# The first hundred microseconds of a spectral-filter and SiLU kernel: other transfers, another order of loads, products of zeros

## The chip, the cores and the metric

The kernel runs on one core of a Trainium2 chip. The metric is the device time of one execution in microseconds; five executions of the kernel before give a median of 2637.14 us (2634.81 to 2638.34). The profile shows one execution. Its engines are TensorE (PE, with its weight loads PEld), VectorE (DVE), ScalarE (ACT), GpSimd (POOL) and SyncE (SP), which here only issues transfers.

## The reference

`x` has 8 batches of 3008 positions and 256 channels. Each batch is filtered in the frequency domain along the positions, and the result goes through a two-layer network:

```python
X = np.fft.rfft(x, axis=1)
Y = X * (filt_r + 1j * filt_i)[None]          # 1505 frequencies x 256 channels
y = np.fft.irfft(Y, n=3008, axis=1).astype(np.float32)
h = y.reshape(24064, 256) @ w_in              # w_in 256 x 2048
out = (h / (1 + np.exp(-h)) @ w_out).astype(np.float32)   # w_out 2048 x 256
```

`x` and the filters are float32. The weights arrive as 64-bit floats (their scale is a float64), and the kernel rounds them itself.

## The kernel before

**The spectral part.** The transform of length 3008 = 47 x 64 is done in stages, each a set of small matrix products with tables (`wf_t`, `d_t`, `e_t`, `wi_t`). For batch 0, and in the same way for batch 1, with other timing:

- `load_x(u)` (L255), for 8 blocks u. A block holds on partitions 0 to 46 and on 64 to 110 the rows 32 apart of both halves of the positions. Each half of a block (`h`) comes in two transfers, of 32 and of 15 rows, all on the Sync queue. Rows 32 to 63 of the tile are filled with zeros first, since `sums` reads rows 0 to 110.
- `sums(u)` (L280): sum and difference of the two halves, two VectorE instructions.
- `stage1(u)` (L294): eight TensorE passes with `wf_t`, two evictions to `t1`, and two writes on GpSimd's queue to the DRAM scratch `d1`. `evac` (L226) gives evictions to ScalarE in batch 0 (`early[0]` is set), and to VectorE and ScalarE in turn after that.
- `load_t2(g)` (L377), for 6 groups g: two transfers on the Sync queue read `d1` back, transposed. All of `d1` has to be written before the first. `forward(g)` (L383) multiplies with `d_t`, and at its end issues the load of group g + 2, as there are two `t2` tiles.
- `multiply(g, k)` (L399) by the filters on VectorE, `add(g, k)` (L408) on GpSimd in batch 0 but for one half of the last group, `inverse(g)` (L414) with `e_t` on TensorE, and then `even` (a ScalarE copy) and `rows` (two VectorE instructions), which writes to the DRAM scratch `d2`, in batch 0 nearly always by ScalarE's queue.
- `load_t4(g)` (L450) reads `d2` back once all of it is written; `stage3(g)` (L456) multiplies with `wi_t`, issues the load of group g + 2 and evicts to `y`.

From batch 2 on the first stage is folded for six of the eight blocks (`load_fold`, `fold`, `stage1_fold`), and only blocks 6 and 7 come by `load_x`.

**The weights.** `load_weights(jp)` (L700) loads two of the 16 columns of 128 hidden units as raw 64-bit words, four transfers of 256 KB. `round_weights(j)` (L714) turns one column into float32: five VectorE and two ScalarE instructions and two GpSimd products, and after every second column four GpSimd combinations.

**The main loop.** 384 steps: 8 batches, two halves each, three runs of tokens each, 8 pairs of hidden columns each. Both layers are multiplied as 2 x 2 blocks with seven products instead of eight. `hidden(step)` (L566) issues the first layer's seven products and the SiLU of one pair, in 8 rounds; `project` (L625) the second layer's products of the step before. The pieces of the next batch's spectral part are placed between them by step and round (`plan`, L487): batch 1's `sums(u)` at step u, round 5, and its `stage1(u)` at step u + 1, round 3. The roundings of columns 9 to 15 lie in steps 0 to 5.

**The order around the change.** The schedule is written by hand: each engine's instructions, and each queue's transfers, stand in the order in which the program calls them (L774 to L861). Transfers of the Sync and ScalarE queues share eight completion counters, and a transfer waits until the previous one on its counter has landed, so at most eight are under way. The start-up of batch 0 (L774 to L819) is: all of x; d_t; raw weights of jp 0; the first third of the filters (Sync queue); the first stage; the rest of the filters (GpSimd's queue); t2 of groups 0 and 1; e_t; two roundings; the six groups; t4; the roundings of columns 4 to 8; four groups of stage 3. Then the main loop's first product is issued (`px`, L579 and L586).

Of the kernel before, what the change touches and what calls it, by code (L numbers as in the profile page):

```python
# [155 lines left out]
def kernel(  # L156
# [47 lines left out]
    f_t = [cpool.tile([128, NG, 2, C], FP32, name=f"filt{i}") for i in range(2)]  # L204

    w_t = cpool.tile([128, 7, 2, NJP, 128], FP32)
    warm = cpool.tile([128, 1], FP32)
    bias_t = cpool.tile([128, 1], FP32)
    x_all = xpool.tile([128, 2, 2, 2 * C], FP32)
# [39 lines left out]
    def spectral(b):  # L249
# [5 lines left out]
        def load_x(u):  # L255


            if b == 0:
                if u == 0:
                    us["t1"] = gpool.tile([128, 2, 2, 2, C], FP32, name="t1_g", tag="g")  # L260
                if u in (0, 2):
                    xs["y"] = ypool.tile([128, 2, HALF], FP32, name=f"x_{b}_{u}", tag="y")
                if u < 4:
                    xs[u] = xs["y"][:, u % 2, 0:1024].rearrange("p (a n) -> p a n", a=2)
                elif u < 6:
                    xs[u] = t4pool.tile([128, 2, 2 * C], FP32, name=f"x_{b}_{u}", tag="t4")
                else:
                    xs[u] = x_t[u % 2]
                (nc.vector, nc.gpsimd)[u % 2].memset(xs[u][32:64], 0.0)
            else:  # L270
                xs[u] = x_t[u % 2]
            for h in range(2):
                for r0, nr in ((0, 32), (32, N1 - 32)):
                    nc.sync.dma_start(
                        out=xs[u][64 * h + r0:64 * h + r0 + nr],
                        in_=bass.AP(tensor=x.tensor,
                                    offset=x.offset + (b * S + 32 * r0 + 4 * u + 2 * h) * C,
                                    ap=[[32 * C, nr], [32 * N1 * C, 2], [1, 2 * C]]))
# [15 lines left out]
        def stage1(u):  # L294
            ut = us.pop(u)
            if b > 0 or u < 2 or u > 5:
                t1 = tpool.tile([128, 2, 2, C], FP32, name=f"t1_{b}_{u}", tag="t")
            elif u < 4:
                t1 = typool.tile([128, 2, 2, C], FP32, name=f"t1_{b}_{u}", tag="ty")
            else:  # L300
                t1 = us["t1"][:, u - 4]
            ps = [bank(b, f"pa_{b}_{u}_{h}") for h in range(2)]
            for par in range(2):
                for h in range(2):
                    rows = slice(64 * h, 64 * h + N1)
                    nc.tensor.matmul(out=ps[h][64 * par:64 * par + 64], lhsT=wf_t[rows, par],  # L306
                                     rhs=ut[rows, par], start=True, stop=True)
            for h in range(2):
                evac(t1[:, h], ps[h])
            for par in range(2):  # L310
                nc.gpsimd.dma_start(
                    out=d1[par].rearrange("s p n c -> (s p) n c")[:, 4 * u:4 * u + 4, :],
                    in_=t1[64 * par:64 * par + 2 * NS].rearrange("p h n c -> p (h n) c"))
# [61 lines left out]
                        in_=us["tf"][32 * k:32 * k + NS].rearrange("p q n c -> p (q n) c"))  # L375

        def load_t2(g):  # L377
            t2s[g] = tpool.tile([128, 4, C], FP32, name=f"t2_{b}_{g}", tag="t")
            for par in range(2):
                nc.sync.dma_start(out=t2s[g][64 * par:64 * par + 64],  # L380
                                  in_=d1[par, 4 * g:4 * g + 4].rearrange("s p n c -> (p n) s c"))

        def forward(g):  # L383
            t2 = t2s.pop(g)
            ps = [bank(b, f"pb_{b}_{g}_{k}") for k in range(2)]
            for ri in range(2):
                for j in range(4):
                    for k in range(2):
                        par, at = slot_source(k, j)
                        rows = slice(64 * par, 64 * par + 64)  # L390
                        nc.tensor.matmul(out=ps[k][32 * j:32 * j + 32, ri, :],  # L391
                                         lhsT=d_t[rows, 4 * g + at, ri, :], rhs=t2[rows, at, :],
                                         start=True, stop=True)
            if g + 2 < NG:
                load_t2(g + 2)
            banks[g] = ps
            prods[g] = []
# [50 lines left out]
                queue.dma_start(out=d2[a0:a0 + 4].rearrange("a n h c -> (a n) h c"), in_=qt[:, a])  # L448

        def load_t4(g):  # L450
            t4s[g] = t4pool.tile([128, 4, C], FP32, name=f"t4_{b}_{g}", tag="t4")
            for h in range(2):
                nc.sync.dma_start(out=t4s[g][64 * h:64 * h + 2 * NS],
                                  in_=d2[:, 4 * g:4 * g + 4, h, :])

        def stage3(g):  # L456
            half, n0 = divmod(4 * g, 16)
            ps = [bank(b, f"pd_{b}_{g}_{h}").rearrange("p a c -> p (a c)")[:, 0:8 * N1]
                  .rearrange("p (a i n) -> p a i n", a=2, i=4) for h in range(2)]
            for cb in range(2):  # L460
                for i in range(4):
                    for c0 in (0, 64):
                        for h in range(2):
                            rows = slice(64 * h, 64 * h + 2 * NS)
                            nc.tensor.matmul(  # L465
                                out=ps[h][c0:c0 + 64, cb, i, :],
                                lhsT=t4s[g][rows, i, 128 * cb + c0:128 * cb + c0 + 64],
                                rhs=wi_t[rows, :], start=True, stop=True)
            if g < 6:
                load_t4(g + 2)  # L470
            if n0 == 0:
                y[b, half] = ypool.tile([128, 2, HALF], FP32, name=f"y_{b}_{half}", tag="y")
            dst = y[b, half].rearrange("p a (r h n) -> p a h n r", h=2, n=16)
            for h in range(2):
                evac(dst[:, :, h, n0:n0 + 4], ps[h])
# [204 lines left out]

    wide = moe_w_in.dtype != FP32
    nc.vector.memset(warm, 0.0)
    nc.scalar.activation(out=warm, in_=warm, func=AFT.Silu)

# [74 lines left out]
    def rounded(j):  # L761
        if wide:
            round_weights(j)
        else:
            load_exact(j)

    def inverse_rows(part, g):
        part["inverse"](g)
        for i in range(2):
# [2 lines left out]


    nc.sync.dma_start(out=wf_t, in_=wf_dram.ap())  # L774
    nc.gpsimd.memset(bias_t, -896.0)
    nc.gpsimd.memset(x_all[96:128], 0.0)
    part = spectral(0)
    for u in range(8):
        part["load_x"](u)
    nc.sync.dma_start(out=d_t, in_=d_dram.ap())  # L780
    weights(0)
    load_filters(nc.sync, 0, 4)
    for u in range(3):
# [1 line left out]
    for u in range(8):  # L785
        part["stage1"](u)
        if u + 3 < 8:
            part["sums"](u + 3)
    load_filters(nc.gpsimd, 4, 2 * NG)
    part["load_t2"](0)  # L790
    part["load_t2"](1)
    nc.sync.dma_start(out=e_t, in_=e_dram.ap())
    rounded(0)
    rounded(1)
    for g in range(NG):
        part["forward"](g)
        if g == 0:
# [7 lines left out]
            part["add"](g, k)  # L805
        if g > 0:
            inverse_rows(part, g - 1)
        if g in (1, 3):
            rounded(2 + g // 2)
    inverse_rows(part, NG - 1)  # L810
    weights(4)
    part["load_t4"](0)
    part["load_t4"](1)
    for j in range(4, 9):
        rounded(j)
        if j == 5:
# [74 lines left out]
```

## Time and profile before

| What | Value |
|---|---|
| Median of five executions | 2637.14 us |
| The profiled execution | 2637.78 us, span 2635.6 us |
| TensorE busy | 2561.2 us, 97% of the span |
| VectorE, ScalarE, GpSimd busy | 1717.0, 1101.1, 491.9 us |
| TensorE busy in the first 120 us | 63.9 us |
| First product of the main loop | at 114.22 us |
| Bytes moved in the first 130 us | 27.35 MB, 210 GB/s on average |
| Mean granted clock of TensorE | 0.987 |

Part 1 of the page gives busy time, share and number of instructions of each engine. Part 2 cuts the span into 40 slices; a digit is the busy share in tenths. A line of the chain of waits has a start, a length and the work or wait that the end was traced back to. A line of the timeline has a start, the length of the whole group, engine, line, operation, tile written and tile read, the count, and in square brackets the idle time before the group with what ended it; `SPq` and `ACTq` are queues issuing transfers. A line of the windows has a stretch, its length, busy time and number of instructions of PE, PEld, DVE, ACT and POOL, the granted clock, the busy share of the 16 DMA engines, and GB/s. Tiles are called by the kernel's names without numbers: `t` is any of `t1`, `t2`, `t4`; `d` is `d1` or `d2`.

The granted clock reads 1.00 from the start, although the eight passes of a first-stage block take 2.48 us at 14.41 us and 1.09 at 134.56; so the column is no measure in the first 60 us.

### The profile page before, as it was taken

The numbers are of one execution on the slowest core, as the hardware profiler recorded it, in microseconds if no ns is written. First come the engines' busy times: TensorE is split into PE (matmuls) and PEld (weight loads), VectorE is DVE, ScalarE is ACT, GpSimd is POOL, SyncE is SP. The second block draws the span as 40 slices with busy tenths as digits, with TensorE's granted clock in tenths as the row PEclk, the third lists the DMA queues.
The fourth block names the chain that finished last, engine by engine and source line by source line (L and its number), as shares of the span: only waits on it lengthen the run. The fifth ranks groups of instructions, "written<-read, shape, count | busy, mean of one in ns | idle before, by whom it ended". The sixth has DMA issues, their size and how long they took to land.

```text
span 2635.6 us, 48160 instructions
## 1 busy us (share of the span) xinstructions
PE 2561.2 (97%) x18720; PEld 2164.0 (82%) x18720; DVE 1717.0 (65%) x3578; ACT 1101.1 (42%) x3012; POOL 491.9 (19%) x742
## 2 busy tenths in 40 slices
PE   4699999999999999999999999999999999999998
PEld 1468888888888888888888888888888888888987
DVE  4886666667666766666666666666666666555554
ACT  2344344444444444444444444444444444444443
POOL 5541112111211121112112211121112111100100
PEclk9599999999999999999999999999999999999999
DMA  9542222322223123222222222232222311210000
GB/s 255 162 120 57 67 60 69 77 54 67 68 71 73 46 63 82 67 65 60 74 61 56 73 71 64 53 82 65 65 56 73 84 45 28 55 22 21 9 16 16
DMA packets 205611, 176.11 MB, mean 67 GB/s; under 512 B 122916, under 2 KB 176932, under 8 KB 204980
## 3 DMA queue, kind: packets, MB, share of 16 engines
q1 hardware_dynamic: 184776, 120.35, 19.1%
q0 software_dynamic: 17936, 49.57, 6.1%
q8 instruction: 147, 2.41, 0.4%
q10 hardware_dynamic: 2672, 3.13, 0.4%
q14 instruction: 80, 0.66, 0.1%
HBM read 97.97 MB, written 84.41 MB: 69 GB/s over the span
## 4 chain that ended last, share of the span: by engine, by line
PE 94%; DVE 2%; DMA 1%; ACT 1%; issue 1%; POOL 0%; ACTq 0%; DVEq 0%; POOLq 0%
PE acc L638 43%; PE px L579 26%; PE pyz L579 18%; PE pd L465 2%; PE pb L391 2%; PE pc L424 2%; PE pf L361 1%; PE pa L306 1%; DMA t<-d 0%; DVE g L550 0%; DVE u L289 0%; DVE work L726 0%; DMA filt<-in_filt_i_dram 0%; DVE work L721 0%; DMA d<-t 0%
## 5 line engine op out<-in xcount | busy, mean ns | idle before, releaser
L638 PE MATMUL acc<-g,w_t 128*128 128x256 f32 (+1 forms) x5376 | 1513.3, 375 | 0.4 <-DVE g L550 0.4
L638 PEld LDWEIGHTS acc<-g,w_t 128*128 128x128 f32 x5376 | 1022.2, 190 | 116.0 <-DVE g L550 0.8
L550 DVE TENSOR_TENSOR g<-pyz,abc 128x256 f32<-128x256 f32 (+1 forms) x1152 | 479.8, 416 | 534.2 <-ACT abc L600 294.5
L550 DVE TENSOR_TENSOR g<-g 128x256 f32<-128x256 f32 (+3 forms) x1152 | 619.3, 538 | 196.7 <-ACT g L583 183.6
L579 PE MATMUL px<-ty,w_t 128*128 128x256 f32 (+1 forms) x2304 | 688.1, 380 | 3.7 <-ACT abc L594 3.3
L583 ACT ACTIVATE g<-g 128x256 f32<-128x256 f32 (+1 forms) x1152 | 473.0, 411 | 247.5 <-DVE g L550 247.5
L550 POOL TENSOR_TENSOR s<-s 128x256 f32<-128x256 f32 (+1 forms) x329 | 259.7, 807 | 1446.3 <-DVE s L656 1435.3
L579 PEld LDWEIGHTS px<-ty,w_t 128*128 128x128 f32 x2304 | 424.4, 190 | 89.0 <-issue 30.7
L579 PE MATMUL pyz<-y,w_t 128*128 128x256 f32 (+1 forms) x1536 | 454.6, 378 | 1.7 <-DVE g L550 1.7
L579 PEld LDWEIGHTS pyz<-y,w_t 128*128 128x128 f32 x1536 | 284.2, 190 | 47.8 <-DVE g L550 6.9
L594 ACT COPY abc<-px 128x256 f32<-128x256 f32 (+1 forms) x384 | 141.3, 368 | 367.2 <-PE px L579 367.2
L583 ACT ACTIVATE g<-px 128x256 f32<-128x256 f32 (+1 forms) x384 | 145.8, 380 | 308.0 <-PE px L579 308.0
L600 ACT COPY abc<-px 128x256 f32<-128x256 f32 (+1 forms) x384 | 143.6, 374 | 311.1 <-PE px L579 310.9
L579 PE MATMUL px<-y,w_t 128*128 128x256 f32 (+1 forms) x768 | 230.7, 382 | 4.6 <-ACT g L583 2.6
L579 PE MATMUL pyz<-ty,w_t 128*128 128x256 f32 (+1 forms) x768 | 225.8, 376 | 0.0
L579 PEld LDWEIGHTS px<-y,w_t 128*128 128x128 f32 x768 | 142.2, 190 | 44.1 <-ACT g L583 15.4
L579 PEld LDWEIGHTS pyz<-ty,w_t 128*128 128x128 f32 x768 | 145.9, 190 | 17.2 <-DVE g L550 0.9
L587 ACT COPY abc<-px 128x256 f32<-128x256 f32 (+1 forms) x384 | 134.9, 351 | 2.7 <-PE px L579 1.3
L230 DVE COPY y<-pd 128x376 f32<-128x376 f32 x60 | 48.4, 806 | 97.6 <-PE pd L465 97.6
L465 PEld LDWEIGHTS pd<-wi_t,t 48*64 48x64 f32 x4096 | 69.6, 140 | 34.5 <-issue 25.0
L465 PE MATMUL pd<-wi_t,t 48*64 48x47 f32 x4096 | 78.0, 239 | 13.5 <-ACT work L725 8.0
L232 ACT COPY y<-pd 128x376 f32<-128x376 f32 x68 | 54.0, 815 | 86.8 <-PE pd L465 86.8
(68 smaller groups left out, 1354.3 us busy)
## 6 DMA issues: line engine op xcount, KB each, us to landing
t<-d SPq DMA_DIRECT2D x96, 256.0 KB
t<-d SPq DMA_DIRECT2D x128, 192.0 KB
d<-q POOLq DMA_DIRECT2D x85, 256.0 KB, 2.6
out_dram<-o SPq DMA_DIRECT2D x636, 32.0 KB
d<-tf POOLq DMA_DIRECT2D x144, 96.0 KB, 2.4
d<-t POOLq DMA_DIRECT2D x52, 192.0 KB, 3.3
xr<-in_x_dram SPq DMA_DIRECT2D x6, 1472.0 KB
x_all<-in_x_dram SPq DMA_DIRECT2D x72, 96.0 KB
```

What stands on the lines that cost most here:

```text
L230: nc.vector.tensor_copy(out=dst, in_=src)
L232: nc.scalar.copy(out=dst, in_=src)
L391: nc.tensor.matmul(out=ps[k][32 * j:32 * j + 32, ri, :], lhsT=d_t[rows, 4 * g + at, ri, :], rhs=t2[rows, at, :], start=True, stop=True)
L424: nc.tensor.matmul(out=ps[j][64 * k:64 * k + 64, a, :], lhsT=e_t[rows, g + a, k, ri, :], rhs=zs[k][rows, ri, :], start=(a == 0 and ri == 0 ...
L465: nc.tensor.matmul(out=ps[h][c0:c0 + 64, cb, i, :], lhsT=t4s[g][rows, i, 128 * cb + c0:128 * cb + c0 + 64], rhs=wi_t[rows, :], start=True, ...
L550: eng.tensor_tensor(out=out, in0=in0, in1=in1, op=op)
L579: nc.tensor.matmul(out=out, lhsT=w_t[:, c, 0, jp], rhs=rhs, start=start, stop=True, skip_group_check=True)
L583: nc.scalar.activation(out=g[:, k, 0:n], in_=g[:, k, 0:n] if src is None else src, func=AFT.Silu)
L587: nc.scalar.copy(out=sums[:, 0, 0:n], in_=xo)
L594: nc.scalar.copy(out=sums[:, 1, 0:n], in_=xo)
L600: nc.scalar.copy(out=sums[:, 2, 0:n], in_=xo)
L638: nc.tensor.matmul(out=acc[pair][i][:, h, 0:n], lhsT=w_t[:, c, 1, jp], rhs=g[:, k, 0:n], start=(jp == 0 and h == 0), stop=last, skip_group ...
```

## The change

- **x.** Each half of a block is one transfer, of 48 rows (47 and one that is not used), and for the first half of blocks 0 and 1 of 64 rows, in place of the zero fill. In batch 0 the second halves go out on ScalarE's queue. All batches but the last use the 48 rows. The fill of `x_all[96:128]` goes.
- **Order of loads.** `d_t` comes in two parts, the second behind t2 of groups 0 and 1; t2 of groups 2 and 3 is loaded ahead too, into t4's tiles; the other two thirds of the filters move from GpSimd's queue to the Sync queue, behind all these.
- **Four t4 tiles.** t4 of groups 2 and 3 is loaded with that of 0 and 1, into the tiles of t2.
- **Products of zeros.** `idle(n)` issues n products of a zero tile into a PSUM tile that nothing reads: 7 ahead of the first stage, 16 ahead of group 0, 2 behind each group, 14 ahead of stage 3.
- **Evictions.** Batch 1's first stage is evicted by ScalarE alone.
- The SiLU that loads ScalarE's table moves behind the first block's transfers.

```diff
 def load_x(u):
-                (nc.vector, nc.gpsimd)[u % 2].memset(xs[u][32:64], 0.0)
+                if u > 1:
+                    (nc.vector, nc.gpsimd)[u % 2].memset(xs[u][32:64], 0.0)
...
             for h in range(2):
-                for r0, nr in ((0, 32), (32, N1 - 32)):
-                    nc.sync.dma_start(
+                more = ((0, 32), (32, N1 - 32))
+                if b < B - 1:
+                    more = ((0, 64 if b == 0 and u < 2 and h == 0 else N1 + 1),)
+                queue = nc.scalar if b == 0 and h == 1 else nc.sync
+                for r0, nr in more:
+                    queue.dma_start(
...
 def stage1(u):
             for h in range(2):
-                evac(t1[:, h], ps[h])
+                if b == 1:
+                    nc.scalar.copy(out=t1[:, h], in_=ps[h])
+                else:
+                    evac(t1[:, h], ps[h])
...
 def load_t2(g):
-            t2s[g] = tpool.tile([128, 4, C], FP32, name=f"t2_{b}_{g}", tag="t")
+            if b == 0 and g in (2, 3):
+                t2s[g] = t4pool.tile([128, 4, C], FP32, name=f"t2_{b}_{g}", tag="t4")
+            else:
+                t2s[g] = tpool.tile([128, 4, C], FP32, name=f"t2_{b}_{g}", tag="t")
...
 def forward(g):
-            if g + 2 < NG:
+            if g + 2 < NG and (b > 0 or g > 1):
                 load_t2(g + 2)
...
 def load_t4(g):
-            t4s[g] = t4pool.tile([128, 4, C], FP32, name=f"t4_{b}_{g}", tag="t4")
+            if b == 0 and g in (2, 3):
+                t4s[g] = tpool.tile([128, 4, C], FP32, name=f"t4_{b}_{g}", tag="t")
+            else:
+                t4s[g] = t4pool.tile([128, 4, C], FP32, name=f"t4_{b}_{g}", tag="t4")
...
 def stage3(g):
-            if g < 6:
+            if g < 6 and (b > 0 or g > 1):
                 load_t4(g + 2)
...
+    def idle(n):
+        ps = xps.tile([128, 512], FP32, name="idle", tag="x")
+        for _ in range(n):
+            nc.tensor.matmul(out=ps[:, 0:256], lhsT=zero_t[:, 0:128], rhs=zero_t, start=True, stop=True)
...
     nc.sync.dma_start(out=wf_t, in_=wf_dram.ap())
+    nc.vector.memset(zero_t, 0.0)
     nc.gpsimd.memset(bias_t, -896.0)
-    nc.gpsimd.memset(x_all[96:128], 0.0)
     part = spectral(0)
     for u in range(8):
         part["load_x"](u)
-    nc.sync.dma_start(out=d_t, in_=d_dram.ap())
+        if u == 0:
+            nc.scalar.activation(out=warm, in_=warm, func=AFT.Silu)
+    idle(7)
+    nc.sync.dma_start(out=d_t[:, 0:8], in_=d_dram[:, 0:8])
     weights(0)
     load_filters(nc.sync, 0, 4)
...
-    load_filters(nc.gpsimd, 4, 2 * NG)
-    part["load_t2"](0)
-    part["load_t2"](1)
+    for g in range(2):
+        part["load_t2"](g)
+    nc.sync.dma_start(out=d_t[:, 8:NS], in_=d_dram[:, 8:NS])
     nc.sync.dma_start(out=e_t, in_=e_dram.ap())
+    for g in range(2, 4):
+        part["load_t2"](g)
+    load_filters(nc.sync, 4, 2 * NG)
     rounded(0)
     rounded(1)
+    idle(16)
     for g in range(NG):
...
         if g > 0:
             inverse_rows(part, g - 1)
+        idle(2)
         if g in (1, 3):
             rounded(2 + g // 2)
     inverse_rows(part, NG - 1)
+    idle(14)
     weights(4)
-    part["load_t4"](0)
-    part["load_t4"](1)
+    for g in range(4):
+        part["load_t4"](g)
```

More of the change, by code (lines that the diff above doesn't have):

```diff
@@ L206 @@
     w_t = cpool.tile([128, 7, 2, NJP, 128], FP32)
+    zero_t = cpool.tile([128, 256], FP32)
     warm = cpool.tile([128, 1], FP32)
@@ L682 @@
     nc.vector.memset(warm, 0.0)
-    nc.scalar.activation(out=warm, in_=warm, func=AFT.Silu)
     PLACES = (((A11, 1), (A11, 2)), ((S3, 1), (A12, 2)))
```

## The prediction

> **What bounds the kernel now.** I read the page's parts 1 and 4 first: TensorE is busy for 97% of the span and makes 94% of the chain. So the time is that of TensorE's work, plus whatever TensorE loses; parts 1 and 2 show the loss at the start. Windows of 20 us put numbers on it: TensorE is busy 20.00 of 20.00 from 180 us on, but only 5 to 13 of 20 in each window before 120. Whatever moves the first product of the main loop (114.22 us, L579) moves the end.
>
> ```profile
> PE 2561.2 (97%) x18720; PEld 2164.0 (82%) x18720; DVE 1717.0 (65%) x3578; ACT 1101.1 (42%) x3012; POOL 491.9 (19%) x742
> PE   4699999999999999999999999999999999999998
> DMA  9542222322223123222222222232222311210000
> ```
>
> The chain of waits and the timeline then give the order of the first 115 us. The last write of the first stage lands at 34.2; the loads of the second stage (L380) are issued from 41.07, because the Sync queue stands behind filter loads; group 0's products start at 49.75; group 2's multiply starts at 64.88. Until there the transfers are the limit. From there to 114.22 it is a chain over VectorE and ScalarE: multiply and add for groups 2 to 5 (a period of 4.86 us), the rounding of five weight columns from 91.67, and only behind that, in ScalarE's own order, the eight evictions of stage 3.
>
> ```profile
> 28.53 5.68 DMA d<-t
> 35.67 6.21 DMA filt<-in_filt_i_dram
> 41.88 7.73 DMA t<-d
> ```
>
> ```profile
> 41.07 3.63 SPq L380 DMA_DIRECT2D t<-d  x4
> 61.09 0.42 DVE L721 TENSOR_SCALAR work<-raw 128x512 uint32<-128x512 uint32 x1
> 64.88 0.68 DVE L403 TENSOR_TENSOR z<-pb,filt 128x512 f32<-128x512 f32 x1
> 108.79 5.37 ACT L232 COPY y<-pd 128x376 f32<-128x376 f32 x8
> 114.22 1.22 PE L579 MATMUL px<-y,w_t 128*128 128x256 f32 x2 [1.97 <-ACT y L232]
> ```
>
> In the next lines the last two columns are the DMA engines' busy share and GB/s. With x alone the engines move 200; with raw weights and first-stage writes 386 (the mean of 27 to 33 us); with filters 203 to 243, at the same share.
>
> ```profile
> 9.00:12.00 3.00, 3.00 (x15) 0.82 (x12) 1.45 (x3) 2.11 (x4) 1.22 (x2) 1.00 1.00 200
> 27.00:30.00 3.00, 0.00 (x0) 0.00 (x0) 0.00 (x0) 0.73 (x2) 1.98 (x4) 1.00 1.05 407
> 42.00:45.00 3.00, 0.00 (x0) 0.00 (x0) 0.00 (x0) 0.00 (x0) 2.92 (x5) 1.00 1.00 203
> ```
>
> **The change, part by part.**
>
> *x by two queues.* Before, 24 issues take 11.38 us, 0.474 each, of 94 KB on average: 198 GB/s, which is what the windows show. So issuing limits x. After, 16 transfers of 192 or 256 KB go out on two queues, 8 each, and issuing would allow four times that. ScalarE issues its 8 (3.8 us) and waits for older ones to land before its first eviction (8.98 before, some 9.5 after); the evictions, 1.07 us a block, end long before their writes land, so this costs nothing. Two of the eight zero fills of 0.91 us and GpSimd's 1.80 for x_all's last rows go, one for the zeros comes: all in time in which VectorE and GpSimd wait for x. ScalarE's table load (1.28) moves behind its first issue, still ahead of that first eviction. In batch 1 half of the 32 issues go, and half of the last blocks' in later batches; the Sync queue's time there hides nothing that TensorE waits for: 0.
>
> *When the second stage can load (T0, 41.07 before).* By then x (3.28 MB), the first-stage writes (16 x 192 KB, 3.15), a third of d_t (0.26), the first raw weights (1.05) and eight of the first 16 filter transfers (0.52; eight may be under way) must have moved. x at the 314 GB/s of 12 to 21 us: 10.4 us. The other 5.06 MB with wf at the 386 of 27 to 33: 13.1. Before 2.5 us nothing moves. T0 = 26.0. Bounds: everything at 386, 24.1; all 16 filters landed and everything at the 321 of 12 to 33 us, 30.1.
>
> *Loads in order of use.* Behind T0 the Sync queue now holds four groups of t2 (2.10 MB), the rest of d_t (0.52), e_t (0.79), the other two thirds of the filters (2.10, before on GpSimd's queue) and only then raw weights of jp 1. VectorE's order has rounded(2) ahead of group 2's multiply, so that multiply waits for the first half of those weights (0.52). Filters with the 0.52 left over, at the 228 GB/s of 33 to 48 us: 11.5 us. The rest with group 0's two writes and two small tables, 4.54 MB at the 310 of 60 to 75: 14.6. Landing 2.6 (part 6 of the page, d<-q). Rounding 2.9 (74.60 to 77.49). Sum 31.6: group 2's multiply at 57.6 instead of 64.88, **7.3 us earlier**. Bounds: all at 310, from the early T0, 52.7 (12.2 earlier); all at 228, from the late T0 and with the 3.8 us that the rounding took from 61.09, 67.9 (3.0 later). In the built program the seventh of these filter transfers waits for a completion counter that it shares with group 0's first write to d2, the ninth for the second write's. From landed t2 (49.6) to that write's issue (62.10) it took 12.5 us; it lands about T0+19.6 to 21.7, and by bytes the queue gets there at T0+19.4: 0 to 2.3 us, taken as 0. GpSimd loses 16 issues of some 0.52 us; its next work is a weight product that nothing reads before 114, so 0.
>
> *After 57.6* the same chain stands, as VectorE's order is unchanged. Next to be late is t2 of groups 4 and 5: at 310 GB/s, behind 2.6 and then 2.1 MB more, they land at 63.1 and 69.9, and their products, 7.3 us earlier than 71.87 and 78.87, want them at 64.6 and 71.6.
>
> *Four t4 tiles.* Loads for groups 2 and 3 no longer wait for stage 3. But the evictions start at 108.79, when ScalarE is through the last rounding (L725, 108.16 for 0.72), and then run back to back. Gain 0 and cost 0; the cover is 16.5 us of rounding.
>
> *Products of zeros.* 49 of them, 0.43 us at full clock (L579, two passes), 0.87 at half. 7 lie before stage 1 (TensorE idle to 6.38), 16 in the idle time 26.6 to 48.4, 14 in 89.6 to 97.6 and, if slower, in the 11 us in which stage 3's evictions wait. The 12 between groups can cost: at half clock a group is 2.41 (L391) + 2.59 (L424) + 1.74, against VectorE's 4.86. I expect the slots before group 5's inverse to matter alone: with a full clock it ends at 88.4 instead of 89.6, and VectorE, free at 89.2, gains **0.8**; with a half clock 1.2 is lost. The row nearest is the 0.85 granted at 75 to 78, after 9 us of dense work, which the products add to: -0.8.
>
> ```profile
> 63.00:66.00 3.00, 0.00 (x0) 0.00 (x0) 2.77 (x5) 1.03 (x3) 0.95 (x2) 0.50 1.08 372
> 75.00:78.00 3.00, 1.40 (x26) 0.77 (x19) 2.52 (x6) 1.50 (x3) 0.35 (x1) 0.85 0.36 137
> ```
>
> [...]
>
> *ScalarE evicts.* Batch 1's first stage runs in steps 1 to 8. There VectorE's copy falls away (0.60) and ScalarE's grows by one, ahead of L600, for which VectorE's next instruction waits:
>
> ```profile
> 136.11 0.57 ACT L232 COPY t<-pa 128x512 f32<-128x512 f32 x1
> 136.74 0.37 ACT L600 COPY abc<-px 128x256 f32<-128x256 f32 x1
> 136.73 0.68 DVE L230 COPY t<-pa 128x512 f32<-128x512 f32 x1
> 137.33 0.41 DVE L550 TENSOR_TENSOR g<-pyz,abc 128x256 f32<-128x256 f32 x1
> ```
>
> L600 moves to 137.3, its reader follows 0.40 later (182.25 to 182.65): 137.70 instead of 137.33. In the five steps with rounding VectorE sets the period, so **+1.8**. Bounds: five times 0.60 gained (-3.0), and 0.4 more in each of the three steps where TensorE is the bound (+3.0).
>
> Sum: -7.3 - 0.8 + 1.8 = -6.3 us on the profiled execution's 2637.8 (span 2635.6), which is 0.6 above the median: **2631.5**, 5.6 under the median of 2637.1. 0.2% (5.3 us) is about what a measurement can tell from no change.
>
> **Rivals.**
>
> *The two queues bring nothing (0.28).* For it: share 1.00 at 200 GB/s from 9 to 12 us may mean full engines. Against: from 3 to 9 us the share is 0.69 to 0.83 at the same rate. Price: x at 200 takes 16.4 us, 6.0 more: 2637.5, no change. [...]
>
> *The smaller parts cost (0.12).* Evictions +3.0 and products +1.2 leave 2634.7: no change. Here the products don't do what they are named for, since the clock stays at half.
>
> *Products become the bound (0.12).* If TensorE stays at half clock from 58 to 90 and nothing hides the 12 products, 10.4 us come on: 2642.7, slower, less if VectorE's 4.86 us hides part. It decides where more than 10 of them are exposed. Against it: rounded(3) gives TensorE 2.9 us of slack, and dense work lifts the clock.
>
> **How the numbers follow.** My case has 0.48; no change 0.40 (the first two rivals), slower 0.12. The range is 2624 to 2641: the fast bound of the loads (-12.2, so 2626.6) with half of what the evictions could gain, and up to 1 us short of the slow one (+3.0, so 2641.8). The likeliest case alone has 2624 to 2632.
>
> **What the next profile shows.** Right: t2 issued near 26, group 2's multiply near 57.6, the main loop's first product near 107; the windows of 3 to 12 us near 300 GB/s; the step in which batch 1's stage 1 lies 0.3 to 0.4 longer. Wrong: 200 GB/s again; VectorE waiting for raw weights past 62; TensorE waiting for nothing between groups 3 and 5; or the steps getting shorter.

## The result, and the profile after

The changed kernel takes 2642.94 us (median of 28 runs, 2640.68 to 2645.23) against 2637.36 (48 runs, 2634.53 to 2641.40): 1.0021 times as long, with a 95% interval of 1.0016 to 1.0026. It is 5.6 us slower; 2631.5 was forecast, and 2641 was the end of the range. Its profiled execution took 2640.26 us (span 2638.5), less than any of its timed runs, so this profile shows one of its shorter executions; what is known of the difference stands below.

The page of the changed kernel, busy times and the slices of the span:

```profile
PE 2575.9 (98%) x18818; PEld 2178.2 (83%) x18818; DVE 1712.1 (65%) x3570; ACT 1104.3 (42%) x3020; POOL 481.1 (18%) x724
...
PE   6699999999999999999999999999999999999998
...
DMA  9632222321223123221222222232122311211000
```

The first slice shows TensorE at 6 where it had 4, but that is not work done: 29.6 us of its busy time in the first 120 us are products of zeros. In the second slice the transfers have 6 instead of 5, in the third 3 instead of 4. The chain of waits of the changed kernel at the start:

```profile
39.02 7.44 DMA e_t<-e_tbl
...
53.02 16.73 issue
69.75 1.03 PE pb L404 x2
```

TensorE stands for 16.7 us. The timeline says for what. (`SPq` rows are issues of the Sync queue; the bracket is the idle time and what ended it.)

```profile
35.58 2.75 SPq L393 DMA_DIRECT2D t<-d  x4
...
54.28 0.62 SPq L220 DMA_DIRECT2D filt<-in_filt_r_dram  x1
54.95 0.60 SPq L220 DMA_DIRECT2D filt<-in_filt_i_dram  x1
...
60.09 0.59 SPq L220 DMA_DIRECT2D filt<-in_filt_i_dram  x1
...
61.88 0.38 SPq L723 DMA_DIRECT2D raw<-in_moe_w_in_dram  x1
...
65.50 0.43 DVE L736 TENSOR_SCALAR work<-raw 128x512 uint32<-128x512 uint32 x1 [14.79 <-DMA raw<-in_moe_w_out_dram]
...
68.36 0.68 DVE L416 TENSOR_TENSOR z<-pb,filt 128x512 f32<-128x512 f32 x1
...
117.97 1.22 PE L595 MATMUL px<-y,w_t 128*128 128x256 f32 x2 [1.94 <-ACT y L233]
```

t2 is issued at 35.58 (T0), 5.5 us earlier than before, but 9.6 later than forecast. Group 2's multiply comes at 68.36, 3.5 us later than before: VectorE waits 14.8 us for raw weights, which stand in the Sync queue behind the filters. From the multiply on all is as before: 49.6 us to the main loop's first product, 49.3 before. Windows of the changed kernel (stretch, length, busy PE, PEld, DVE, ACT, POOL, clock, share of the transfer engines, GB/s):

```profile
9.00:12.00 3.00, 3.00 (x20) 0.78 (x16) 2.44 (x4) 0.00 (x0) 0.00 (x0) 1.00 1.09 176
27.00:30.00 3.00, 3.00 (x9) 2.37 (x8) 2.44 (x6) 1.24 (x2) 1.82 (x4) 0.50 1.05 407
54.00:57.00 3.00, 0.00 (x0) 0.00 (x0) 0.00 (x0) 0.00 (x0) 0.00 (x0) 1.00 0.38 115
57.00:60.00 3.00, 0.00 (x0) 0.00 (x0) 0.00 (x0) 0.00 (x0) 0.00 (x0) 0.57 0.70 199
75.00:78.00 3.00, 2.96 (x49) 1.50 (x48) 2.13 (x6) 0.52 (x2) 2.45 (x4) 1.00 1.09 348
```

x moves slower than before (176 against 200 in the first line), with the engines at a share of 1.09 against 1.00. From 54 to 60 they are partly idle (0.38 and 0.70), and nothing computes: the Sync queue issues ten filter transfers of 128 KB, one every 0.64 us, which is some 200 GB/s.

**What is known of the 5.6 us.** The profiled execution is only 2.9 us longer than the one before (spans of 2638.5 and 2635.6): the first product comes 3.75 later, and 1.0 is won back where a spell of half clock is missing (0.50 from 168.03 to 171.45 before, 1.00 from 125 to 200 in the changed kernel). The 12.67 us from one first-stage block to the next at 160.56 to 173.23 before are 11.67 in the changed kernel (164.15 to 175.82). This has nothing to do with the change, as far as the runs show: the same interval takes 11.6 to 11.7 us in eight of the 18 profiled kernels and 12.4 to 13.0 in the other ten, with either kind of eviction in both lots. The kernel of experiment e4 (below) is the same up to step 1, so its profile shows this start a second time: multiply at 69.65, first product at 119.25, 5.0 later than before, and 13.02 us for the interval. Its 1.28 us more at the start and 1.35 more in the interval are near the 2.7 by which the changed kernel's profiled execution lies under its median. So a start some 5 us late fits the 5.6. How often each start comes, one profile of each kernel cannot say.

### The profile page after: what moved, and what is told of

Its sections match the earlier page's. It is cut to its first block, busy times and chain, and to the rows that moved or that the text cites. A ratio compares the mean times of both kernels' runs of the same rounds, so it can differ in the third digit from the quotient of the medians.

```text
span 2638.5 us, 48260 instructions
## 1 busy us (share of the span) xinstructions
PE 2575.9 (98%) x18818; PEld 2178.2 (83%) x18818; DVE 1712.1 (65%) x3570; ACT 1104.3 (42%) x3020; POOL 481.1 (18%) x724
## 4 chain that ended last, share of the span: by engine, by line
PE 93%; DVE 2%; DMA 1%; issue 1%; ACT 1%; SPq 0%; POOL 0%; ACTq 0%; DVEq 0%; POOLq 0%
PE acc L654 42%; PE px L595 25%; PE pyz L595 18%; PE pd L481 2%; PE pc L437 2%; PE pb L404 2%; PE pf L371 1%; PE pa L313 1%; DMA x_all<-in_x_dram 0%; DVE u L296 0%; DMA raw<-in_moe_w_out_dram 0%; DVE g L566 0%; DMA x<-in_x_dram 0%; DMA e_t<-e_tbl 0%; DVE q L456 0%
```

## The experiments

Theory at the outset: the loss lies behind T0, in one queue that has to issue everything in order, and x on two queues brings no rate. Rivals: the bytes, whatever the queue; the products of zeros; the evictions. Every kernel here computes the whole result. Of each kernel with 11 runs the ratio to before is known to about 0.0009 either way (2.4 us), so the medians don't settle differences of 1 us between two of them. Nor does the time at which something starts in a single profile: the same start differs by 1.28 us between the changed kernel and e4. For these the text goes by what waits for what, and by the length of one stretch.

### Each part undone in the changed kernel: e1 to e4

**e1.** The second filter part on GpSimd's queue again.

```diff
-    load_filters(nc.sync, 4, 2 * NG)
+    load_filters(nc.gpsimd, 4, 2 * NG)
```

> The changed kernel with one move undone: the other two thirds of the filters go out on GpSimd's queue again, at the same place in the order. Theory (the Sync queue holds them up: 0.64 us an issue, a stall on shared counters, and the raw weights behind them): raw weights of jp 1 are issued near 45 to 50 instead of 61.88, and group 2's multiply comes at 58 to 64 instead of 68.36; time 2633 to 2638. Rival (the bytes hold it up, whatever the queue): multiply within 1.5 us of 68.36, time 2641 to 2643.

Measured: 2645.86 us, 1.0032 (1.0019 to 1.0045); multiply at 72.69. Neither: slower still. The raw weights were issued at 52.63, 9 us earlier than in the changed kernel, if later than the theory's 45 to 50. But the timeline of e1 shows a new wait:

```profile
68.59 0.37 ACT L448 COPY q<-pc 128x256 f32<-128x256 f32 x1 [10.01 <-DMA t<-d]
...
68.99 0.88 DVE L456 TENSOR_TENSOR q<-q,pc 128x256 f32<-128x256 f32 x2 [9.51 <-ACT q L448]
```

ScalarE, in its own order, had to issue group 0's write to d2 (ready near 59.5). By the first bracket (10.01 us, ended by `t<-d`) that write waits until t2 of group 4, issued on the Sync queue at 62.34, has landed: they have the same completion counter. VectorE's `rows` stands behind ScalarE's next copy, the rounding of column 2 behind `rows`. The first wait went, another took its place.

**e2.** All 16 transfers of x on the Sync queue.

```diff
-                queue = nc.scalar if b == 0 and h == 1 else nc.sync
+                queue = nc.sync
```

> The changed kernel with all 16 transfers of x on the Sync queue. Theory (the transfer engines are full with x alone, the second issuer brings no rate and only keeps ScalarE from its first evictions): first eviction near 9 to 10 instead of 14.05, last block of x no later, t2 issued within 1.5 us of 35.58, time 2641 to 2644. Rival (two queues at once slow the transfers down): 300 GB/s again from 12 us on, t2 issued at 30 to 33, time 2637 to 2641.

Measured: 2641.78 us, 1.0013 (1.0004 to 1.0022). First eviction at 8.55, the last block's sum at 20.16 instead of 22.27, t2 issued at 34.25; in the windows of 3 to 15 us 240, 223, 228 and 222 GB/s, against 218, 195, 176 and 150. One queue moves x faster than two, so the theory's "brings no rate" was too mild. The multiply came at 68.59 all the same: the filters and raw weights of the Sync queue ended at the same time, so the earlier start bought nothing.

**e3.** No products of zeros.

```diff
-        for _ in range(n):
+        for _ in range(0):
```

> The changed kernel without its products of zeros (the zero tile is still filled). Theory (they neither help nor cost): 2642 to 2644. Rival 1 (they take time from group 5's inverse or throttle the clock later): 2638 to 2641. Rival 2 (they shorten the half-clocked start of the main loop): 2645 to 2648.

Measured: 2641.60 us, 1.0014 (1.0005 to 1.0023), between the theory and rival 1. The profile of e3 shows the first product at 118.00, where the changed kernel has it (117.97), and the next steps as well (step 1's first stage at 129.27, against 129.24). From the multiply to the first product it is 49.59 us without the products and 49.61 with them. They help nothing that the profile shows. Whether they cost the 1.3 us of the medians stays open.

**e4.** Both engines evict batch 1's first stage.

```diff
-                if b == 1:
-                    nc.scalar.copy(out=t1[:, h], in_=ps[h])
-                else:
-                    evac(t1[:, h], ps[h])
+                evac(t1[:, h], ps[h])
```

> The changed kernel with batch 1's first stage evicted by VectorE and ScalarE in turn again. Theory (in the profile the steps with rounding are as long as before on average, those bound by TensorE 0.2 longer): 2642 to 2643.5. Rival (the prediction's term, 0.37 in five steps): 2640.5 to 2641.5.

Measured: 2642.15 us, 1.0019 (1.0010 to 1.0028). In the steps with rounding the two profiles have the same periods to 0.02 us (8.92, 8.74, 8.53, 8.72 in the changed kernel, 8.91, 8.73, 8.53, 8.74 in e4). In the steps that TensorE bounds the changed kernel takes 7.48, e4 7.26. First e4's first-stage products there, then the changed kernel's:

```profile
178.46 1.09 PE L313 MATMUL pa<-u,wf_t 47*64 47x512 f32 x8
185.72 1.09 PE L313 MATMUL pa<-u,wf_t 47*64 47x512 f32 x8
```

```profile
175.82 1.09 PE L313 MATMUL pa<-u,wf_t 47*64 47x512 f32 x8
183.30 1.09 PE L313 MATMUL pa<-u,wf_t 47*64 47x512 f32 x8
```

Two such intervals lie in the profiles and make 0.45 us; a third step as long would make the theory's 0.7. The median is 0.8 lower, which is within what the runs can tell.

### Queue, counter or bytes: e5 to e8

**e5.** Group 0's two writes to d2 on GpSimd's queue, so that no filter transfer shares a counter with them; nothing else.

```diff
-                queue = nc.gpsimd if b > 0 or (g == NG - 1 and i == 0) else nc.scalar
+                queue = nc.gpsimd if b > 0 or g == 0 or (g == NG - 1 and i == 0) else nc.scalar
```

> The changed kernel with group 0's two writes to d2 on GpSimd's queue, so that no filter transfer of the Sync queue shares a completion counter with them. Theory (the second filter part waits for that write, then is issued one by one at 0.64 us, and the raw weights stand behind it): the 16 filter issues of L220 run from 43 to 57.5 instead of 60.1 to 61.3, raw weights of jp 1 are issued near 59, group 2's multiply comes near 66 instead of 68.4 to 69.7; time 2639 to 2640.5. Rival (the wait on the counter only hides full transfer engines): multiply at 68 to 69.7, time 2642 to 2643.

Measured: 2639.84 us, 1.0013 (1.0004 to 1.0022), 3.1 us under the changed kernel. The stall of 2.6 us before the seventh filter is down to 0.8; the last is issued at 58.70, the multiply comes at 67.34 (the theory said near 66):

```profile
58.70 0.59 SPq L220 DMA_DIRECT2D filt<-in_filt_i_dram  x1
...
64.47 0.43 DVE L736 TENSOR_SCALAR work<-raw 128x512 uint32<-128x512 uint32 x1 [12.54 <-DMA raw<-in_moe_w_out_dram]
```

Against 60.09 in the changed kernel and 61.29 in e4 the shared counter costs 1.4 to 2.6 us of the queue's time.

**e6.** As e5, and raw weights of jp 1 ahead of the second filter part.

```diff
-    load_filters(nc.sync, 4, 2 * NG)
     rounded(0)
     rounded(1)
+    weights(1)
+    load_filters(nc.sync, 4, 2 * NG)
```

> As the run with group 0's d2 writes on GpSimd's queue, and the raw weights of jp 1 ahead of the second filter part. Theory (order and issue rate of one queue): VectorE no longer waits for raw weights; group 2's multiply waits for the last filters, which land near 64; the rounding's 2.9 us lie ahead of that; multiply near 64, time 2636.5 to 2638. Rival (bytes): multiply at 67 or later, time 2641 to 2643.

Measured: 2640.15 us, 1.0013 (1.0004 to 1.0022). The multiply came at 63.85, where the theory put it, but the time did not follow. In e6's timeline the first bracket names `wi_t`, which shares a counter with one of the filters; the multiply reads the filters.

```profile
63.85 0.69 DVE L416 TENSOR_TENSOR z<-pb,filt 128x512 f32<-128x512 f32 x1 [8.93 <-DMA wi_t<-wi_tbl]
...
77.33 0.63 ACT L737 ACTIVATE work<-work 128x512 f32<-128x512 uint32 x1 [4.50 <-DMA d<-q]
```

ScalarE stands at a d2 write again (issued at 76.91), and the first product comes 52.7 us behind the multiply (116.51), not 49.6.

**e7.** e1 and e5 together: filters and group 0's d2 writes on GpSimd's queue.

> The first experiment (second filter part on GpSimd's queue) again, with group 0's d2 writes on GpSimd's queue too. Theory (in that run ScalarE stood 10 us behind a counter that its d2 write shared with the t2 load of group 4; without it the raw weights, issued at 52.6 to 57.0, are the last to come): ScalarE's wait is gone, group 2's multiply at 62 to 64, time 2635 to 2637.5. Rival (filters and t2 in each other's way cost as much as the queue saves): multiply at 67 or later, time 2641 or more.

Measured: 2639.79 us, 1.0010 (1.0002 to 1.0019); multiply at 64.12, 8.6 us earlier than in e1 by one queue for two writes. So e1's slowness was the counter. The time stayed above the theory's, since group 1's d2 write now stands behind t2 of group 4:

```profile
69.32 0.37 ACT L448 COPY q<-pc 128x256 f32<-128x256 f32 x1 [6.05 <-DMA t<-d]
```

**e8.** The first third of the filters behind t2 of groups 0 and 1.

```diff
-    load_filters(nc.sync, 0, 4)
...
     for g in range(2):
         part["load_t2"](g)
+    load_filters(nc.sync, 0, 4)
```

> The changed kernel with the first third of the filters issued behind t2 of groups 0 and 1. Theory (T0 was set by the 16 issues of 0.64 us ahead of it, not by bytes): t2 issued at 30 to 32.5 instead of 35.6, when the last first-stage write has landed; what this does to the end is open, as the filters then come later: 2640 to 2645. Rival (x and the writes set T0): t2 issued at 34 or later.

Measured: 2648.11 us, 1.0044 (1.0030 to 1.0058). T0 came at 32.66, just outside the theory's 32.5: the 16 issues held it up by 2.9 us, x and the writes set the rest. The 16 issues, 10.3 us, then stood ahead of all the rest: `e_t` was issued 7.3 us later than in the changed kernel, group 0's products waited 10.4 us for it, and the multiply came at 74.95, 6.6 us later.

### One part alone, in the kernel before: b1, b2, f1

**b1.** x in 16 transfers, all on the Sync queue.

```diff
-                for r0, nr in ((0, 32), (32, N1 - 32)):
+                more = ((0, 32), (32, N1 - 32))
+                if b < B - 1:
+                    more = ((0, 64 if b == 0 and u < 2 and h == 0 else N1 + 1),)
+                for r0, nr in more:
```

> The kernel before with x alone changed: 16 transfers of 192 or 256 KB, all on the Sync queue. Theory (fewer, larger transfers raise x from 200 to about 225 GB/s, as in the changed kernel with one queue): t2 issued 1 to 2.5 us before 41.07, group 2's multiply as much before 64.88, time 2635 to 2636.5. Rival (the Sync queue's filter issues set the time of t2 in any case): 2637 to 2638.

Measured: 2634.77 us, 0.9991 (0.9982 to 1.0000): 2.9 us under before, at the edge of what is told apart. T0 35.36, better than expected (5.7 earlier), multiply 61.24, first product 110.48.

**b2.** The same by two queues, as in the changed kernel (`queue = nc.scalar if b == 0 and h == 1 else nc.sync`, and the SiLU behind the first block).

> The kernel before with x alone changed, in 16 transfers by two queues (and the SiLU that loads ScalarE's table behind the first block's). Compared with the same 16 transfers by one queue (t2 issued at 35.36, 2634.8). Theory (two issuers move x slower than one, 150 to 218 GB/s against 222 to 240 in the two profiles of the changed kernel): windows of 6 to 15 us below 200 GB/s, first eviction at 13 to 14.5, t2 issued 1 to 2 us later than with one queue, time 2636 to 2637.5. Rival (the slow x was due to the products or to the order of the rest): 2634 to 2635.5, 220 GB/s or more.

Measured: 2637.44 us, 1.0000 (0.9991 to 1.0008). T0 37.09, multiply 65.07. The windows of 3 to 9 us, in which only x moves, first of b1, then of b2:

```profile
3.00:9.00 6.00, 2.17 (x10) 0.73 (x12) 3.22 (x6) 0.00 (x0) 2.46 (x3) 1.00 0.98 248
```

```profile
3.00:9.00 6.00, 0.97 (x6) 0.58 (x8) 2.33 (x4) 0.00 (x0) 2.47 (x3) 1.00 1.07 205
```

From 9 to 15 us b2 moves 167 GB/s at share 1.08. And ScalarE is held at its issues, as b2's timeline shows (in b1 the first eviction is at 9.44):

```profile
14.10 3.04 ACT L232 COPY t<-pa 128x512 f32<-128x512 f32 x6 [11.43 <-DMA x<-in_x_dram]
```

The last block's sum is at 17.80 in b1 and at 23.84 in b2. So in these profiles the second queue costs all that the larger transfers bring; the two medians, 2.7 us apart, agree.

**f1.** The second filter part on the Sync queue, behind t2 of groups 0 and 1 and `e_t`.

```diff
-    load_filters(nc.gpsimd, 4, 2 * NG)
     part["load_t2"](0)
     part["load_t2"](1)
     nc.sync.dma_start(out=e_t, in_=e_dram.ap())
+    load_filters(nc.sync, 4, 2 * NG)
```

> The kernel before with the second filter part alone moved: from GpSimd's queue to the Sync queue, behind t2 of groups 0 and 1 and e_t. (t2 of group 2, which stands behind it there, moves too.) Theory (this move is what costs the changed kernel its gain: 16 issues of 0.64 us and a stall behind group 0's d2 write lie between t2 and the raw weights): t2 issued earlier than 41.07, as GpSimd's filters are out of the way, at 36 to 39, but raw weights of jp 1 at 62 or later and group 2's multiply at 68 to 74; time 2641 to 2647. Rival (the bytes up to group 2 set the time, in whatever order): multiply within 2 us of 64.88, 2636 to 2639.

Measured: 2644.63 us, 1.0024 (1.0015 to 1.0034): this move alone costs 7.1 us (before took 2637.55 in the same runs). T0 comes 2.5 us earlier (38.61), the multiply 6.9 later (71.79), by the same wait as in the changed kernel:

```profile
64.14 0.38 SPq L708 DMA_DIRECT2D raw<-in_moe_w_in_dram  x1
...
68.92 0.43 DVE L721 TENSOR_SCALAR work<-raw 128x512 uint32<-128x512 uint32 x1 [13.23 <-DMA raw<-in_moe_w_out_dram]
```

### Put together: c0 to c4

**c0.** The changed kernel with four parts undone: filters and group 0's d2 writes as in e7, x as in e2, no products, evictions as in e4.

> The changed kernel with four of its parts undone together: second filter part on GpSimd's queue (with group 0's d2 writes), x on one queue, no products of zeros, batch 1's first stage evicted by both engines. What stays: 16 transfers of x, t2 of four groups loaded ahead, d_t in two parts, four t4 tiles. Theory (the losses found one by one add up: 3.1, 1.2, 1.3 and 0.8 us by the runs so far): 2636 to 2637.5, level with the kernel before. Rival (they hide behind one another): 2638 to 2640.

Measured: 2635.65 us, 0.9994 (0.9985 to 1.0003). So these four parts account for the loss: without them the kernel is level with before. That the rest costs nothing isn't shown, since it holds b1's larger transfers, worth 2.9 us alone, and in c0 ScalarE stands 7.6 us at t2 of group 4 again.

**c1.** c0, with the filters issued by two queues and the raw weights early.

```diff
-    load_filters(nc.sync, 0, 4)
+    load_filters(nc.sync, 0, 4, (0,))       # real half
...
+    load_filters(nc.gpsimd, 0, 4, (1,))     # imaginary half, behind the first-stage writes
     for g in range(2):
         part["load_t2"](g)
...
     rounded(1)
+    weights(1)
```

(d2 writes of groups 0 and 1 by GpSimd.)

> The kernel with four parts undone, and: of the first filter part the real half on the Sync queue ahead of t2, the imaginary half on GpSimd's queue behind the first-stage writes; the rest of the filters on GpSimd's queue; raw weights of jp 1 on the Sync queue right behind t2 of group 3; d2 writes of groups 0 and 1 on GpSimd's queue. Theory (the Sync queue's issues and their order were what held group 2 up): t2 issued at 28.5 to 30.5, group 2's multiply at 57 to 61, time 2629 to 2633. Rival (the bytes up to group 2 hold it up): t2 early, multiply at 63 or later, 2635 or more.

Measured: 2635.06 us, 0.9991 (0.9982 to 1.0000). T0 29.07, 6.5 us before the changed kernel's; multiply 61.30, between the two theories; no better than b1. From 30 to 57 us the transfer engines have share 0.86 to 1.13 at 208 to 273 GB/s. But the long wait ahead of group 2 is another: VectorE waits 0.4 us for raw weights and 11.5 us for group 0's additions on GpSimd, as c1's timeline shows:

```profile
53.29 0.69 DVE L413 TENSOR_TENSOR p<-pb,filt 128x512 f32<-128x512 f32 x1 [11.52 <-POOL z L422]
```

GpSimd was at its filter issues until 46.0, most of the later ones behind an earlier transfer that had to land, and at weight products and combinations until 51.9. So in c1 transfers under way held up the issues, and the issues a compute engine.

**c2.** c1, with groups 4 and 5's filters in a part of their own, behind group 1's additions on GpSimd's queue.

> As the run with the filters shared by both queues, and the rest of the filters in two parts: groups 2 and 3 behind the first part, groups 4 and 5 behind the additions of group 1 on GpSimd's queue (16 more issues of half the size). Theory: 1.05 MB less ahead of group 2, its multiply 2 to 4 us earlier than with one part, time 2627 to 2631. Rival (GpSimd's 8 us of further issues hold up its additions or the d2 writes): no earlier, 2632 or more.

Measured: 2643.44 us, 1.0021 (1.0012 to 1.0030); one of its 11 runs took 4493 us, which nothing here explains. Multiply at 58.05, the earliest of all, but GpSimd was at its issues from 54.5 to 70.2, and VectorE waited 9.6 us for group 2's additions: the rival.

**c3.** c2, with that part on the Sync queue behind t2 of group 4, and raw weights of jp 2 and 3 one group later.

> As the run with the rest of the filters in two parts, but groups 4 and 5's part on the Sync queue, behind t2 of group 4, and raw weights of jp 2 and 3 one group later. Theory (1.05 MB less ahead of group 2, and nothing of it on GpSimd's queue): group 2's multiply at 56.5 to 59, no wait of VectorE over 5 us behind it, time 2630 to 2633. Rival (the late half, at 0.64 us an issue, now holds up group 4 or the next raw weights): multiply as early, but a wait of 3 us or more at group 4 or at column 4's rounding, time 2634 or more.

Measured: 2635.75 us, 0.9991 (0.9982 to 1.0000). Multiply at 58.99, as the theory said. That the 1.05 MB less ahead of it did this isn't shown: c4, with the same order up to there, has 60.94, and c1 61.30. In all of c1 to c4 VectorE waits 9.9 to 11.6 us for GpSimd's first additions. The rival was right on what came next, at another place, group 2's d2 write (c3's timeline):

```profile
72.27 0.37 ACT L445 COPY q<-pc 128x256 f32<-128x256 f32 x1 [6.61 <-DMA raw<-in_moe_w_in_dram]
```

**c4.** c3, with group 2's d2 writes on GpSimd's queue too (`g < 3`).

> As the run with groups 4 and 5's filters on the Sync queue, and group 2's d2 writes on GpSimd's queue too, so that ScalarE no longer waits there 6.6 us for raw weights of jp 2. Theory (that wait took what the early multiply had won): group 2's multiply at 58 to 60 again, the main loop's first product 49.3 to 50 behind it, at 107.5 to 110, time 2630.5 to 2633.5, below both kernels. Rival (the next wait stands behind it: group 4's filters or column 4's raw weights): first product at 111 or later, 2634 or more.

Measured: 2633.51 us, 0.9982 (0.9973 to 0.9991): 4.1 us under the kernel before and 9.4 under the changed one. Multiply at 60.94, first product at 111.60. The time is the theory's upper end, the first product lies where the rival had it, as the wait has moved on to group 3:

```profile
78.96 0.37 ACT L445 COPY q<-pc 128x256 f32<-128x256 f32 x1 [7.30 <-DMA raw<-in_moe_w_in_dram]
```

### All runs side by side

| Kernel | us | t2 issued | Group 2's multiply | First product |
|---|---|---|---|---|
| before | 2637.36 | 41.07 | 64.88 | 114.22 |
| changed | 2642.94 | 35.58 | 68.36 | 117.97 |
| e1 filters by GpSimd | 2645.86 | 36.72 | 72.69 | 122.36 |
| e2 x by one queue | 2641.78 | 34.25 | 68.59 | 118.55 |
| e3 no products | 2641.60 | 35.13 | 68.41 | 118.00 |
| e4 both evict | 2642.15 | 35.34 | 69.65 | 119.25 |
| e5 d2 of group 0 by GpSimd | 2639.84 | 35.38 | 67.34 | 116.71 |
| e6 and raw weights first | 2640.15 | 35.00 | 63.85 | 116.51 |
| e7 e1 and e5 | 2639.79 | 35.91 | 64.12 | 114.98 |
| e8 first filters late | 2648.11 | 32.66 | 74.95 | 124.91 |
| c0 four undone | 2635.65 | 36.30 | 62.61 | 115.37 |
| b1 before, x in 16 | 2634.77 | 35.36 | 61.24 | 110.48 |
| b2 the same, two queues | 2637.44 | 37.09 | 65.07 | 114.38 |
| f1 before, filters by Sync | 2644.63 | 38.61 | 71.79 | 122.88 |
| c1 filters shared | 2635.06 | 29.07 | 61.30 | 110.38 |
| c2 filters by use | 2643.44 | 28.61 | 58.05 | 118.14 |
| c3 the same by Sync | 2635.75 | 29.59 | 58.99 | 113.05 |
| c4 and d2 of group 2 | 2633.51 | 29.68 | 60.94 | 111.60 |

An early T0 alone decides nothing: c1 to c4 have it near 29, b1 at 35, and b1 is level with c1. Where neither a ScalarE wait nor, in c2, GpSimd's late additions intervene, the first product follows the multiply by 49.1 to 50.0 us.

## Why the prediction was wrong, step by step

*What bounds the kernel* was right: the time follows the main loop's first product, and that follows group 2's multiply.

*x by two queues* is the step that failed. It took 314 GB/s for x from windows (12 to 21 us of before) in which first-stage writes and raw weights moved too; the windows with x alone showed 200, and share 1.00 in one of them. Measured: 207 GB/s from 3 to 9 us, 163 from 9 to 15. By the forecast x was through at 12.9 us; its last block's sum came at 22.27. One queue does 231 and 225 there (e2), with writes from 9.9 on. That issuing held x up before was right as far as b1 shows: 16 transfers raise 200 GB/s at share 0.76 (before, 3 to 9 us) to 248 at 0.98 (b1), well short of 314. The forecast wanted 8.3 MB moved by 26.0; the windows add up to 5.6. Where x was through, the rate was what the forecast had taken (369 to 407 from 21 to 33 us, taken 386). So most of T0's 9.6 us is x's rate; 2.9 are the 16 filter issues ahead of t2 (e8), which the forecast counted as bytes alone. The other kernels fit: T0 is 29.07 in c1, with x on one queue and half of these issues on GpSimd's, 32.66 in e8, with two queues and none of these issues, and 35.58 here, so 3.1, 3.6 and 2.9 us. That ScalarE's issues cost nothing was wrong by 5 us of first evictions (14.05 against 8.98), since it was held there until older transfers landed. b2, with the second queue, moved 43 GB/s less than b1 from 3 to 9 us (205 against 248).

*Loads in order of use* came out near in sum and wrong in its terms. Multiply at T0 + 31.6 forecast, T0 + 32.8 measured. But it reckoned the queue by bytes at 228 to 310 GB/s; in fact ten filters went at 0.64 us each with the engines at 0.38 and 0.70 (54 to 60 us), after a stall on the shared counter that was seen in the program and taken as 0 (1.4 to 2.6 us, e5). That the issues set the pace there, the rows from 54.28 to 60.09 show. The loss against before lies in this step, and the forecast had nearly all of it: it says that T0 to multiply grows from 23.8 to 31.6, which only an early T0 could pay for. f1 measured that part alone: 7.1 us slower.

*After the multiply the same chain*: right (49.6 against 49.3). *Four t4 tiles*: right, first eviction at 112.59, 5.38 ahead of the first product, as before (5.43).

*Products of zeros* (-0.8): they brought a full clock from 75 to 78 us (1.00, against 0.50 in e3), but that did not move group 5 or the main loop's start; 0 by the profiles of e3 and the changed kernel. Nor did they become the bound. That dense work lifts the clock, on which the term and the answer to the third rival rested, the kernel before shows at 75.87 us: 0.50 became 1.00 after two stretches of 3.41 us in which TensorE was busy throughout, though not after the first of them. At the rise at 123.66 the stretch of 3.41 us ahead had 3.23 us of work, the two before that, from 113.42 on, 2.61 and 2.49. The changed kernel has 0.50 from 57.40 to 74.47 and 1.00 from there to 84.71, so not the half clock from 58 to 90 that the third rival took.

*ScalarE evicts* (+1.8): right in sign, wrong in place. The wait that was foreseen is there, in the changed kernel's timeline:

```profile
139.71 1.06 ACT L317 COPY t<-pa 128x512 f32<-128x512 f32 x2
...
140.66 0.39 ACT L616 COPY abc<-px 128x256 f32<-128x256 f32 x1
141.08 0.42 DVE L566 TENSOR_TENSOR g<-pyz,abc 128x256 f32<-128x256 f32 x1 [0.66 <-ACT abc L616]
```

But VectorE lost a copy of 0.6 in the same step and waits 0.66 instead: 0 in the steps with rounding. The cost is 0.22 in each step that TensorE bounds, for which the upper bound had 0.4: 0.7 if there are three. The sum doesn't show it: from the fifth first-stage block to the eighth it is 26.61 to 27.66 us with ScalarE alone and 26.96 to 27.54 with both engines. The interval behind the fifth block alone differs by more than the 0.7: 12.67 us before, with 3.42 us at 0.50 in it, and 11.67 in the changed kernel, with none.

*The rivals.* "The two queues bring nothing" (2637.5, chance 0.28) had the mechanism, and stopped short: it took 200 GB/s where two queues did 163 to 207, and had no price for issues. From its sum, T0 3.6 later than its 32.0, the multiply 1.2 later than T0 + 31.6, no gain by products (0.8) and 1.1 less for evictions give 2642.0. The slower side was put on products of zeros; it came from the Sync queue. In the range its upper end stood on the slow bound of the loads, which took a T0 of 30.1 as the latest.

## What to carry to other kernels

Take a transfer's rate only from windows in which nothing else moves, and price a queue twice, by bytes and by issues: the larger one counts. When transfers are moved to another queue, ask what then stands behind them in order, and which later transfers, of the Sync or the ScalarE queue, share a completion counter with them: ScalarE, which issued such a transfer in e1, stood 10.01 us with it. And before taking a gain at the front of a chain, check the length of the rest of the chain against it, part by part, in one kernel each.

## What the runs showed of the hardware

- Two queues issuing the same 16 transfers of x moved it slower than one: 205 against 248 GB/s from 3 to 9 us, at an engine share of 1.07 against 0.98 (b2, b1). With shares over 1.0 the windows here moved from 150 (1.06, from 12 to 15 us of the changed kernel) to 412 GB/s (1.05, from 18 to 21 us of e2), so here the share says little of the rate. The cause isn't known; whether it is the second queue as such, or that other pieces of x are then under way together, no run separates.
- A filter transfer mostly took 0.59 to 0.62 us of issuing on the Sync queue (the changed kernel, 64 KB from 27 to 36 us and 128 KB from 54 to 61) and 0.49 to 0.56 on GpSimd's (before, 128 KB, from 29 to 42). One issue of raw weights lasted 8.30 us in c1 (at 39.42), at shares of 1.01 to 1.11.
- In the traces of both kernels every issue of the Sync and ScalarE queues (1330 before, 1295 in the changed kernel) carries one of eight completion counters. Before, the ninth issue, at 4.68 us, waits on the counter of the first, at 0.74; in the changed kernel the filter transfer at 54.28 waits on that of ScalarE's write to d2 at 49.03. ScalarE, which issues a few writes between its copies, stood 4.5 to 10.0 us at shared completion counters in e1, e6, e7, c0, c3 and c4. Which transfers share one changed with every edit of the order, so a wait taken away at one group came back at another.
- TensorE's granted clock fell after a stretch of 3.42 us in which TensorE was busy for 2.48 (before, at 62.22). It rose after stretches of 3.41 us with 3.41 (before, at 75.87; changed, at 74.47), 3.23 (before, at 123.66) and 2.99 (changed, at 122.26), and not after one with 3.41 (before, at 72.46) and those with 2.61 and 2.49 (before, from 113.42).
